# Forming three weight gradients per 512-token chunk between attention units, with fp32 sums in DRAM

## The chip, the cores and the metric

The kernel runs on one core of a Trainium2 chip. The metric is the device time of one execution, in microseconds (us). The kernel before takes 3382.19 us (median of 3 runs, 3378.85 to 3383.56). Runs of the same kernel in one job agree within about 0.3%. Between jobs the median of the kernel before ranged from 3380.52 to 3388.10 us, so times of different jobs are compared only where the difference is well above 8 us.

## The reference, cut to what matters

The kernel computes an adaptive-layernorm transformer block, its output and nine gradients. The sequence has 2048 tokens, the width is 512, there are 32 heads of 16, and the dense layer has 1792 hidden units.

```python
h = layernorm(x) * (1 + ca) + sa
x = x + ga * attention(h, wqkv, wo)
h = layernorm(x) * (1 + cb) + sb
x = x + gb * (relu(h @ w1 + b1) ** 2 @ w2 + b2)
# outputs: x and the gradients of A_x, wqkv, wo, w1, b1, w2, b2, c, w_mod
```

The change concerns the gradients of `wo` (output 3), `w1` (output 4) and `w2` (output 6). Each is a sum over all 2048 tokens.

## The kernel before

Forward attention is a list of 512 units: 4 query chunks of 512 tokens, 8 head groups, 16 key tiles. A unit is two pairs of score matmuls, two exponentials on ScalarE (ACT) and four matmuls with V ("PV"). Matmul results land in PSUM, in the profile lines below as tiles of 128x512 or 128x1024 fp32; a tile of 128x512 fills what I call one bank, and another engine has to copy it out ("evict" it) before the bank can be used again. When all head groups of a chunk are done, that chunk's dense forward and backward become a generator, and one step of it is put behind each unit of the next chunk. The last chunk's generator has no attention to hide behind; I call its run "the tail". "Stage J" is the stage that follows backward attention.

```python
pools["s"]  = tile_pool(name="psS", bufs=3, PSUM)   # scores, 2 banks each
pools["o"]  = tile_pool(name="psO", bufs=1, PSUM)   # PV sums
pools["mm"] = tile_pool(name="psM", bufs=1, PSUM)   # all dense work: one bank
with tc.manual_schedule(engines={PE.engine, ACT.engine}):
    for u in range(NF + 6):
        fscore(u)                 # scores and two exponentials
        fpv(u - 2)                # PV
        if dense:                 # one step of the chunk before
            if wait > 0: wait -= 1
            else: wait = next(dense[0], -1) ...
        # ffinish(...): normalise a finished chunk, start its generator
```

The dense steps store token-major copies of their operands (`gf_st`, `h2_st`, `da_st`, `stok_st`, `dztok_st`) in DRAM. After the tail comes a stage of its own:

```python
# load all stored operands; build padded, transposed weights for stage J
for t3 in range(3):
    for hg in range(HG):
        ...   # in all 96 small copies on ScalarE's DMA queue
        ACT.dma_start(out=wT_bld[o0:o0 + DH, ...], in_=tmpT[r0:r0 + DH, :])
for fc in range(FC):              # likewise for wo and w1
    acc = psg.tile([P, 512], F32, name="aw", tag="aw")
    for t in range(TT):           # sum over all 16 token tiles in PSUM
        PE.matmul(acc[:], sz["s", t // 4][:, fc, t % 4, :], toks["gf"][:, t, :],
                  start=(t == 0), stop=(t == TT - 1))
    acc_out(fc, wblk[:], acc[:])
    SP.dma_start(out=out_6[fc * P:(fc + 1) * P, :], in_=wblk[:])
```

Backward attention follows, then stage J, which uses the padded weights `wT_pad`.

## Time and profile before

The span of 3386.2 us splits as follows. The landmarks are the first score matmul, the last PV matmul, the first load for backward attention, and the last matmul of backward attention's dQ.

| stretch | us |
|---|---|
| preparation, to the first score | 287.1 |
| forward attention, first score to last PV | 991.8 |
| tail: dense work of the last chunk alone | 147.7 |
| weight-gradient stage, to the first backward load | 189.2 |
| backward attention | 1463.9 |
| the rest (stage J and the end) | 306.5 |

The first view is the busy-time windows of the kernel before. Columns: the window, the busy us of PE (TensorE), its weight load, DVE (VectorE), ACT and POOL (GpSimd), each with a count of instructions, then the granted clock, the DMA share and GB/s.

```profile
600.00:650.00 50.00, 44.78 (x313) 14.60 (x314) 18.67 (x33) 50.00 (x55) 8.45 (x7) 1.00 0.58 128
650.00:700.00 50.00, 45.57 (x304) 14.60 (x305) 21.50 (x55) 49.25 (x54) 11.84 (x23) 0.97 0.73 190
1500.00:1550.00 50.00, 13.39 (x49) 5.58 (x50) 2.08 (x3) 2.72 (x5) 0.00 (x0) 0.58 0.31 97
```

In the first two windows, attention with dense steps between units, ACT has almost no gap; TensorE is nearly as full. In the third, which holds the longest wait of the weight-gradient stage, every engine idles most of the time; over the whole stage TensorE is busy 115.8 of 189.2 us.

The chain of waits of the kernel before in a dense stretch (start, length, what) shows the second limit. L387 is the dense matmul group, L392 its eviction from PSUM.

```profile
590.12 0.76 DVE rT L392
590.88 0.04 issue
590.92 1.04 PE pm L387 x4
591.96 0.02 issue
591.99 0.76 DVE rT L392
```

One turn of the single dense bank is matmuls 1.04, a hand-over, eviction 0.76, a hand-over: 1.87 us from 590.12 to 591.99. That is as long as ACT's two exponentials, so one dense step per unit just fits.

The waits of the kernel before in the weight-gradient stage (who waits for whom: us in total, times, longest):

```profile
ACT wblk L641 <- DMA wT_bld<-tmpT: 80.5, 1, 80.5
PE aw L655 <- ACT wblk L641: 50.7, 1, 50.7
```

and its timeline there:

```profile
1448.82 16.28 PE L648 MATMUL aw<-da_g,O_g 128*128 128x512 bf16 x63 [41.64 <-DMA wT_bld<-tmpT]
...
1483.41 52.40 ACTq L636 DMA_DIRECT2D wT_bld<-tmpT  x80
```

TensorE waited 41.64 us for its first matmul of the stage. Later an eviction on ACT stood behind 80 small DMA issues (52.40 us; 16 of the 96 had gone out earlier), and TensorE waited 50.7 us for it.

The group of exponentials in forward attention, from the costliest groups (busy, mean ns, then the idle time ahead of them and what ended most of it):

```profile
L523 ACT ACTIVATE ET<-psST 128x1024 bf16<-128x1024 f32 x1024 | 945.5, 1311 | 34.7 <-PE psST L521 34.5
```

ACT waited only 34.5 us for scores in the whole forward attention.

### The profile page before, as it was taken

The page shows a single profiled execution, that of the slowest core. Times are in us where ns is not written, and L with a number is a line of the kernel's source. Part 1 is how long each engine was busy: PE and PEld are TensorE (multiplying, and loading weights), DVE is VectorE, ACT ScalarE, POOL GpSimd, SP SyncE. Part 2 cuts the span into 40 slices and gives each one's busy share as a digit, 9 for nine tenths or more (in the row PEclk, how much of TensorE's full clock was granted, in tenths as well). Part 3 has the DMA queues.
Part 4 walks back from the last instruction along what each step waited for, and adds up shares of the span by engine and source line. Part 5 has one row for each costly group of instructions (what it writes and reads, how often), then busy time and mean ns, then how long its engine had stood idle before and what let it go on. Part 6 is the DMA issues. An engine that isn't in the chain of part 4 may idle for free.

```text
span 3386.2 us, 47396 instructions
## 1 busy us (share of the span) xinstructions
PE 2663.9 (79%) x17485; PEld 788.3 (23%) x17549; DVE 1932.1 (57%) x2770; ACT 2157.3 (64%) x3474; POOL 372.3 (11%) x345
## 2 busy tenths in 40 slices
PE   2778998888888885348697889898898978885746
PEld 1232111221221222114122222222222222222312
DVE  8852002332343344400587878788887878884772
ACT  0006999999999992000586878787787868784202
POOL 3000001121121132300110010101010101010000
PEclk7986555975975976778788878888878889897867
DMA  3124001661662654763999999999999999997113
GB/s 128 55 107 150 29 29 47 136 173 52 138 166 57 137 155 100 167 211 115 219 200 213 199 211 197 207 205 204 208 198 209 198 215 201 201 201 182 63 62 94
DMA packets 1388742, 511.31 MB, mean 151 GB/s; under 512 B 1321939, under 2 KB 1359575, under 8 KB 1386205
## 3 DMA queue, kind: packets, MB, share of 16 engines
q1 hardware_dynamic: 1368782, 502.51, 70.8%
q10 hardware_dynamic: 19728, 5.77, 0.8%
q8 instruction: 138, 2.26, 0.3%
q14 instruction: 94, 0.77, 0.1%
HBM read 112.29 MB, written 74.08 MB: 55 GB/s over the span
## 4 chain that ended last, share of the span: by engine, by line
PE 36%; DMA 21%; ACT 18%; DVE 12%; issue 6%; SPq 3%; ACTq 2%; POOL 0%; DVEq 0%; POOLq 0%
DMA dsT<-dS_u 16%; ACT ET L523 14%; PE psS_u L724 7%; PE dqacc L776 5%; ACT E_u L726 4%; PE accVK L761 3%; PE ppad L266 3%; PE accVK L752 2%; PE psST L521 2%; DVE dS_u L738 2%; PE psS_x L724 2%; PE pm L387 2%; ACTq L636 1%; PE pm L420 1%; PE pm L403 1%
## 5 line engine op out<-in xcount | busy, mean ns | idle before, releaser
L738 DVE TENSOR_TENSOR dS_u<-psD_u,E_u 128x1024 bf16<-128x1024 f32 x1024 | 1189.4, 1218 | 248.5 <-PE psD_u L736 166.5
L726 ACT ACTIVATE E_u<-psS_u 128x512 bf16<-128x512 f32 x1536 | 866.3, 633 | 307.2 <-PE psD_u L736 274.0
L523 ACT ACTIVATE ET<-psST 128x1024 bf16<-128x1024 f32 x1024 | 945.5, 1311 | 34.7 <-PE psST L521 34.5
L724 PE MATMUL psS_u<-ik,iq 32*128 32x512 bf16 x1536 | 517.2, 434 | 27.0 <-DVE KS_tok L677 19.1
L521 PE MATMUL psST<-qt_sb,kt_sb 32*128 32x512 bf16 x2048 | 464.6, 507 | 85.2 <-ACT ET L523 37.7
L736 PE MATMUL psD_u<-iv,ido 32*128 32x512 bf16 x2048 | 448.4, 432 | 18.9 <-DVE dS_u L738 11.4
L776 PE MATMUL dqacc<-dsT,KS_tok 128*32 128x512 bf16 x2048 | 212.7, 503 | 161.0 <-DMA dsT<-dS_u 149.2
L726 ACT ACTIVATE E_u<-psS_x 128x512 bf16<-128x512 f32 x512 | 333.9, 652 | 2.2 <-PE psD_u L736 1.7
L537 PE MATMUL oacc<-ET,vaug 128*32 128x512 bf16 x2048 | 270.4, 517 | 0.6 <-ACT ET L523 0.6
L541 DVE COPY ostage<-oacc 128x512 f32<-128x512 f32 x32 | 22.0, 688 | 373.6 <-PE oacc L537 373.6
L761 PE MATMUL accVK<-E_u,dOs_tok 128*16 128x512 bf16 x2048 | 226.3, 432 | 0.0
L724 PE MATMUL psS_x<-ik,iq 32*128 32x512 bf16 x512 | 210.6, 411 | 0.6
L521 PEld LDWEIGHTS <-kt_sb 32*128 32x128 bf16 x2048 | 91.4, 96 | 461.7 <-issue 456.8
L724 PEld LDWEIGHTS <-iq 32*128 32x128 bf16 x2048 | 99.1, 93 | 378.6 <-issue 378.0
L736 PEld LDWEIGHTS <-ido 32*128 32x128 bf16 x2048 | 124.8, 93 | 228.4 <-issue 203.7
L791 POOL TENSOR_TENSOR dQacc<-dQacc,dqtmp 128x512 f32<-128x512 f32 x64 | 81.1, 1268 | 843.0 <-ACT dqtmp L786 843.0
L641 ACT ACTIVATE wblk<-aw 128x512 bf16<-128x512 f32 x9 | 5.4, 597 | 229.4 <-PE aw L648 125.2
L752 PE MATMUL accVK<-dS_u,qz_12652 128*32 128x512 bf16 x1024 | 113.1, 430 | 6.8 <-ACT vkb L764 5.8
L752 PE MATMUL accVK<-dS_u,qz_12651 128*32 128x512 bf16 x1024 | 112.0, 427 | 7.0 <-ACT vkb L764 6.1
L266 PE MATMUL ppad<-xn1T,wpadT 128*128 128x512 bf16 x376 | 98.7, 408 | 21.8 <-DVE stagep L269 16.2
L850 ACT ACTIVATE dqkv_tok<-ptq 128x64 bf16<-128x64 bf16 x128 | 28.6, 224 | 119.8 <-PE ptq L844 119.8
L776 PEld LDWEIGHTS <-KS_tok 128*32 128x32 bf16 x2048 | 52.1, 105 | 221.2 <-issue 179.0
(1021 smaller groups left out, 2496.9 us busy)
## 6 DMA issues: line engine op xcount, KB each, us to landing
kt_sb<-KtP SPq DMA_DIRECT2D x32, 512.0 KB, 3.7
dsT<-dS_u SPq DMA_TRANSPOSE x512, 5.1
wA<-in_B_w_dram SPq DMA_DIRECT2D x4, 1792.0 KB, 8.8
wB<-in_B_w_dram SPq DMA_DIRECT2D x4, 1792.0 KB, 7.7
stok_st<-tk SPq DMA_DIRECT2D x12, 512.0 KB, 3.0
dztok_st<-tk SPq DMA_DIRECT2D x12, 512.0 KB, 4.0
QtP<-stagep SPq DMA_DIRECT2D x8, 512.0 KB, 2.8
KtP<-stagep SPq DMA_DIRECT2D x8, 512.0 KB, 2.9
```

The costliest lines, as they stand in the source:

```text
L266: PE.matmul(pp[:], wpadT[:, ic, which, hg, :], h1T[:, ic, qc * 512:(qc + 1) * 512], start=(ic == 0), stop=(ic == DC - 1))
L521: PE.matmul(ps[:, hi, :], kt_sb[r:r + 32, kt * P:(kt + 1) * P], qt_sb[r:r + 32, :], start=True, stop=True, tile_position=(r, 0))
L523: ACT.activation(ET[:, 2 * pair:2 * pair + 2, :], ps[:], AF.Exp, scale=SCALE)
L537: PE.matmul(oacc[32 * hq:32 * hq + 32, :], lhsT, ET[:, hq, :], start=(kt == 0), stop=(kt == TT - 1), tile_position=(0, 32 * hq), skip_grou ...
L724: PE.matmul(psS[:], st["q"][r:r + 32, qt * P:(qt + 1) * P], st["k"][r:r + 32, kc * 512:kc * 512 + 512], start=True, stop=True, tile_positi ...
L726: ACT.activation(bst[u][0][:, hq, :], psS[:], AF.Exp, scale=SCALE)
L736: PE.matmul(psD[:, hi, :], st["do"][r:r + 32, qt * P:(qt + 1) * P], st["v"][r:r + 32, kc * 512:kc * 512 + 512], start=True, stop=True, til ...
L738: DVE.tensor_tensor(dS_u[:, 2 * pair:2 * pair + 2, :], psD[:], E_u[:, 2 * pair:2 * pair + 2, :], ALU.mult)
L752: PE.matmul(cur["vk"][32 * hq:32 * hq + 32, :], hst[hg]["qz"][:, qt, hq, :], bst[u][1][:, hq, :], start=(qt == 0), stop=False, tile_positi ...
L761: PE.matmul(acc[32 * hq:32 * hq + DH, :], dOs_tok[:, qt, (hg * 4 + hq) * DH:(hg * 4 + hq + 1) * DH], E_u[:, hq, :], start=False, stop=(qt ...
L776: PE.matmul(acc[32 * hq:32 * hq + 32, :], KS_tok[:, kc * 4 + kt, h * DH:h * DH + 32], tT[:, :, hq * 4 + kt, :], start=(kt == 0), stop=(kt ...
L791: POOL.tensor_tensor(dst2, dst, tmp[:], ALU.add)
```

## The change

The intent is to delete the weight-gradient stage. Each chunk's share of the three gradients is formed as 34 "pieces" (14 for `w2`, 16 for `w1`, 4 for `wo`) of 4 matmuls. They stand between the attention units, while operands are still in SBUF. Chunk 0 stores each piece in DRAM as fp32. Chunks 1 and 2 add to it by an accumulating DMA. Chunk 3, in the tail, loads the sum, adds its own share and writes the output. The padded weights of J come from 16 DMA transposes at the start of backward attention. Cut to its core:

```diff
+        def later(f, *args):
+            pend.append((clock[0] + 5, f, args))
+        def dw_piece(c, i, dst, ops, w):
+            if c == QC - 1:
+                part = wk.tile([P, 512], F32, name="dwp", tag="dwp", bufs=3)
+                SP.dma_start(out=part[:, 0:w], in_=dw_st[i][:, 0:w])
+            acc = mm()
+            for ti in range(4):
+                PE.matmul(acc[:, 0:w], ops[ti][0], ops[ti][1], start=(ti == 0), stop=(ti == 3))
+            if c == QC - 1:
+                res = wk.tile([P, 512], BF, name="dwr", tag="ta")
+                DVE.tensor_tensor(res[:, 0:w], acc[:, 0:w], part[:, 0:w], ALU.add)
+                SP.dma_start(out=dst, in_=res[:, 0:w])
+            else:
+                part = wk.tile([P, 512], F32, name="dwp", tag="dwp", bufs=3)
+                DVE.tensor_copy(part[:, 0:w], acc[:, 0:w])
+                if c == 0:
+                    POOL.dma_start(out=dw_st[i][:, 0:w], in_=part[:, 0:w])
+                else:
+                    POOL.dma_start(out=dw_st[i][:, 0:w], in_=part[:, 0:w], accum_op=ALU.add)
...
                 if fc % 4 == 3 or fc == FC - 1:
-                    to_tokens(sT, stok_st[c], fc // 4 * 4, fc + 1)
+                    tk = to_tokens(sT, f0, fc + 1)          # DMA transpose, no store
+                    for f in range(f0, fc + 1):
+                        later(dw_piece, c, DC + f, out_6[...], ..., D)
...
+                    clock[0] = u
+                    stepped = False
+                    if dense and wait == 0:
+                        stepped = True
+                        wait = next(dense[0], -1)
...
+                    if pend and pend[0][0] <= u and not open_group[0] and (not stepped or len(pend) > 2):
+                        _, f, args = pend.pop(0)
+                        f(*args)
...
-            for _ in vaug_left:
-                pass
+            while dense:                                    # the tail
+                for _ in dense.pop(0):
+                    if pend and not open_group[0]:
+                        _, f, args = pend.pop(0)
+                        f(*args)
...
-    (the whole weight-gradient stage)
...
+        for j in range(16):                                 # start of backward attention
+            SP.dma_start(out=wT_pad[:, j, :], in_=wpad_st[:, j * P:(j + 1) * P], transpose=True)
```

Not shown: longer-lived token-major tiles, four `tk` buffers instead of two, and the padded weights that are written to `wpad_st` during preparation.

More of the change, by code (lines that the diff above doesn't have):

```diff
@@ L90 @@
     dOs_st = dram.tile([P, TT, D], BF, name="dOs_st")
-    da_st = dram.tile([P, TT, D], BF, name="da_st")
-    h2_st = dram.tile([P, TT, D], BF, name="h2_st")
-    gf_st = dram.tile([P, TT, D], BF, name="gf_st")
     q_st = dram.tile([P, TT, QPAD], BF, name="q_st")
     k_st = dram.tile([P, TT, QPAD], BF, name="k_st")
-    stok_st = dram.tile([QC, P, 4 * FF], BF, name="stok_st")
-    dztok_st = dram.tile([QC, P, 4 * FF], BF, name="dztok_st")
-    wT_st = dram.tile([P, 16, D], BF, name="wT_st")
+    dw_st = dram.tile([DC + FC + 16, P, 512], F32, name="dw_st")
+    wpad_st = dram.tile([D, 16 * P], BF, name="wpad_st")
     QtP = dram.tile([HG, P, n], BF, name="QtP")
@@ L163 @@
             POOL.tensor_copy(dst, src)
+    wpadVK = wqkvpool.tile([P, DC, HG, 4, 2, DH], BF, name="wpadVK")
+    for ic in range(DC):
+        for t in (1, 2):
+            POOL.tensor_copy(wpadVK[:, ic, :, :, 2 - t, :],
+                             wqkv_nat[:, ic, t * 512:(t + 1) * 512].rearrange("p (hg h d) -> p hg h d", hg=HG, h=4))
+    wpad_v = wpad_st.rearrange("(ic p) c -> p ic c", p=P)
+    SP.dma_start(out=wpad_v[:, :, 0:HG * P], in_=wpadT[:, :, 0].rearrange("p i g c -> p i (g c)"))
+    SP.dma_start(out=wpad_v[:, :, HG * P:], in_=wpadVK.rearrange("p i g h v d -> p i (g h v d)"))
     sa_bc = modbc[:, 0, :]
@@ L321, in load_wB @@
             return w
+        pend, clock, open_group = [], [0], [False]
+        def later(f, *args):
[18 more added lines that the diff above has]
+                    POOL.dma_start(out=dw_st[i][:, 0:w], in_=part[:, 0:w], accum_op=ALU.add)
         def dense_chunk(c, O_c, act):
@@ L334, in dense_chunk @@
             SP.dma_start(out=OT.rearrange("p t o q -> p (t o) q"), in_=flat(O_c), transpose=True)
-            gf_c = cb.tile([P, 4, D], BF, name="gf_c", tag="hd")
+            gf_c = cb.tile([P, 4, D], BF, name="gf_c", tag="gf")
             POOL.tensor_tensor(gf_c[:], g_c[:], gb_bc.unsqueeze(1).to_broadcast([P, 4, D]), ALU.mult)
-            SP.dma_start(out=gf_st[:, ts, :], in_=gf_c[:])
             gfT = cb.tile([P, 4, DC, P], BF, name="gfT", tag="gfT")
@@ L370, in dense_chunk @@
                                   modcol[:, 4, ic:ic + 1], modcol[:, 3, ic:ic + 1], ALU.mult, ALU.add)
-            h2_c = cb.tile([P, 4, D], BF, name="h2_c", tag="hd")
+            h2_c = cb.tile([P, 4, D], BF, name="h2_c", tag="h2")
             POOL.tensor_tensor(h2_c[:], xn2_c[:], cb1_bc.unsqueeze(1).to_broadcast([P, 4, D]), ALU.mult)
             POOL.tensor_tensor(h2_c[:], h2_c[:], sb_bc.unsqueeze(1).to_broadcast([P, 4, D]), ALU.add)
-            SP.dma_start(out=h2_st[:, ts, :], in_=h2_c[:])
             yield 10
@@ L377, in dense_chunk, with to_tokens @@
             sT = cb.tile([P, FC, 512], BF, name="sT", tag="sT")
-            def to_tokens(src, dst, f0, f1):
-                tk = cb.tile([P, 16, P], BF, name="tk", tag="tk", bufs=2)
-                SP.dma_start(out=tk[:, 0:4 * (f1 - f0), :], in_=flat(src[:, f0:f1, :]), transpose=True)
-                SP.dma_start(out=dst[:, 512 * f0:512 * f1], in_=flat(tk[:, 0:4 * (f1 - f0), :]))
+            def to_tokens(src, f0, f1):
+                tk = cb.tile([P, 4, 4, P], BF, name="tk", tag="tk", bufs=4)
+                SP.dma_start(out=tk.rearrange("p f t q -> p (f t) q")[:, 0:4 * (f1 - f0), :], in_=flat(src[:, f0:f1, :]), transpose=True)
+                return tk
             for fc in range(FC):
@@ L394, in dense_chunk @@
                 if fc % 4 == 3 or fc == FC - 1:
-                    to_tokens(sT, stok_st[c], fc // 4 * 4, fc + 1)
+                    f0 = fc // 4 * 4
+                    tk = to_tokens(sT, f0, fc + 1)
+                    for f in range(f0, fc + 1):
+                        later(dw_piece, c, DC + f, out_6[f * P:(f + 1) * P, :],
+                              [(tk[:, f - f0, ti, :], gf_c[:, ti, :]) for ti in range(4)], D)
                 yield 0
@@ L404, in dense_chunk @@
                     if fc % 4 == 3:
+                        open_group[0] = True
                         yield 0
+                open_group[0] = False
                 PE.matmul(pf[:], ones_bf[0:1, 0:P], b2row[0:1, :], start=False, stop=True)
@@ L426, in dense_chunk @@
                 if fc % 4 == 3 or fc == FC - 1:
-                    to_tokens(dzT, dztok_st[c], fc // 4 * 4, fc + 1)
+                    f0 = fc // 4 * 4
+                    nf = fc + 1 - f0
+                    tk = to_tokens(dzT, f0, fc + 1)
+                    for ic in range(DC):
+                        later(dw_piece, c, DC + FC + 4 * (f0 // 4) + ic, out_4[ic * P:(ic + 1) * P, f0 * P:(fc + 1) * P],
+                              [(h2_c[:, ti, ic * P:(ic + 1) * P], tk[:, 0:nf, ti, :]) for ti in range(4)], nf * P)
                 yield 0
             yield 1
-            dx1_c = cb.tile([P, 4, D], BF, name="dx1_c", tag="od")
-            da_c = cb.tile([P, 4, D], BF, name="da_c", tag="hd")
+            dx1_c, da_c = g_c, a_c
             for ti in range(4):
@@ L438, in dense_chunk @@
                     if fc % 4 == 3:
+                        open_group[0] = True
                         yield 0
+                open_group[0] = False
                 xn2 = xn2_c[:, ti, :]
@@ L459, in dense_chunk @@
                                          op0=ALU.mult, op1=ALU.add)
-                DVE.tensor_tensor(da_c[:, ti, :], dx1_c[:, ti, :], ga_bc, ALU.mult)
                 proda = wk.tile([P, D], BF, name="proda", tag="tc")
                 DVE.tensor_tensor(proda[:], dx1_c[:, ti, :], a_c[:, ti, :], ALU.mult)
+                DVE.tensor_tensor(da_c[:, ti, :], dx1_c[:, ti, :], ga_bc, ALU.mult)
                 rowsum(3, proda[:], t)
@@ L467, in dense_chunk @@
             SP.dma_start(out=daT.rearrange("p t o q -> p (t o) q"), in_=flat(da_c), transpose=True)
-            SP.dma_start(out=da_st[:, ts, :], in_=da_c[:])
-            dOs_c = cb.tile([P, 4, D], BF, name="dOs_c", tag="od")
+            dOs_c = cb.tile([P, 4, D], BF, name="dOs_c", tag="x1_c")
             dOp = flat(cb.tile([P, FC, 512], BF, name="dOp", tag="sT"))[:, 0:4 * HG * P]
@@ L472, in dense_chunk @@
             POOL.memset(dOp, 0.0)
+            for oc in range(DC):
+                later(dw_piece, c, oc, out_3[oc * P:(oc + 1) * P, :],
+                      [(O_c[:, ti, oc * P:(oc + 1) * P], da_c[:, ti, :]) for ti in range(4)], D)
             yield 8
@@ L490, in dense_chunk @@
                 if ti % 2 == 1:
-                    dOT = cb.tile([P, 16, P], BF, name="dOT", tag="tk", bufs=2)
+                    dOT = cb.tile([P, 16, P], BF, name="dOT", tag="tk", bufs=4)
                     SP.dma_start(out=dOT[:], in_=dOp[:, ti - 1:ti + 1].rearrange("p t g c -> p (t g c)"), transpose=True)
@@ L539, in fpv @@
             if kt == TT - 1:
-                ostage = wk.tile([P, 512], F32, name="ostage", tag="ostage")
+                ostage = wk.tile([P, 512], F32, name="ostage", tag="ostage", bufs=1)
                 DVE.tensor_copy(ostage[:], oacc[:])
@@ L581 @@
                         fpv(u - 2)
-                    if dense:
-                        if wait > 0:
-                            wait -= 1
-                        else:
-                            wait = next(dense[0], -1)
-                            if wait < 0:
-                                dense.pop(0)
-                                wait = 0
-                    if fdone and (u - 2 >= fdone[0][0] or u == NF + 5):
+                    clock[0] = u
[3 more added lines that the diff above has]
+                        wait = next(dense[0], -1)
+                        if wait < 0:
+                            dense.pop(0)
+                            wait = 0
+                    elif wait > 0:
+                        wait -= 1
+                    if pend and pend[0][0] <= u and not open_group[0] and (not stepped or len(pend) > 2):
+                        _, f, args = pend.pop(0)
+                        f(*args)
+                    if not open_group[0] and fdone and (u - 2 >= fdone[0][0] or u == NF + 5):
                         ffinish(*fdone.pop(0)[1:])
-        vaug_left = dense.pop(0)
-        assert not dense
         with ExitStack() as ph2:
             pools["mm"] = ph2.enter_context(tc.tile_pool(name="psM2", bufs=8, space=bass.MemoryType.PSUM))
-            for _ in vaug_left:
-                pass
-            prows = wk.tile([1, D], F32, name="prows", tag="prows")
+            while dense:
[3 more added lines that the diff above has]
+                        f(*args)
+            for _, f, args in pend:
+                f(*args)
             for j, row in ((0, 5), (1, 3), (2, 4), (3, 2)):
@@ L601 @@
                 PE.matmul(pr[0:1, :], onesf[:, 0:1], racc[:, j, :], start=True, stop=True)
-                prows = wk.tile([1, D], F32, name="prows", tag="prows")
+                prows = wk.tile([1, D], F32, name="prows", tag="dwp", bufs=3)
                 DVE.tensor_copy(prows[:], pr[0:1, :])
@@ L609 @@
     vaugpool.release()
-    with ExitStack() as ph:
-        big = ph.enter_context(tc.tile_pool(name="phG", bufs=1))
-        wk = ph.enter_context(tc.tile_pool(name="phGw", bufs=2))
-        psg = ph.enter_context(tc.tile_pool(name="psG", bufs=8, space=bass.MemoryType.PSUM))
-        toks = {}
-        for key, src in (("gf", gf_st), ("O", o_st), ("da", da_st), ("h2", h2_st)):
-            toks[key] = big.tile([P, TT, D], BF, name=f"{key}_g")
-            SP.dma_start(out=toks[key][:], in_=src[:])
-        sz = {}
-        for key, src in (("s", stok_st), ("dz", dztok_st)):
-            for c in range(QC):
-                sz[key, c] = big.tile([P, FC, 4, P], BF, name=f"{key}{c}", tag="szc", bufs=6)
-                SP.dma_start(out=sz[key, c].rearrange("p f t q -> p (f t q)"), in_=src[c])
-        wT_bld = big.tile([P, 16, D], BF, name="wT_bld")
-        POOL.memset(wT_bld[:], 0.0)
-        for t3 in range(3):
-            for hg in range(HG):
-                if hg % 2 == 0:
-                    tmpT = wk.tile([P, D], BF, name="tmpT", tag="tmpT")
-                    SP.dma_start(out=tmpT[:], in_=A_wqkv[:, (t3 * 4 + hg // 2) * P:(t3 * 4 + hg // 2 + 1) * P], transpose=True)
-                for hq in range(4):
-                    r0 = (hg % 2) * 64 + hq * DH
-                    o0 = 32 * hq + (DH if t3 == 1 else 0)
-                    ACT.dma_start(out=wT_bld[o0:o0 + DH, (0 if t3 == 0 else 8) + hg, :], in_=tmpT[r0:r0 + DH, :])
-        ACT.dma_start(out=wT_st[:], in_=wT_bld[:])
-        def acc_out(i, dst, acc):
-            if i % 2 == 0:
-                ACT.activation(dst, acc, AF.Identity)
-            else:
-                DVE.tensor_copy(dst, acc)
-        for oc in range(DC):
-            acc = psg.tile([P, 512], F32, name="aw", tag="aw")
-            for t in range(TT):
-                PE.matmul(acc[:], toks["O"][:, t, oc * P:(oc + 1) * P], toks["da"][:, t, :], start=(t == 0), stop=(t == TT - 1))
-            wblk = wk.tile([P, D], BF, name="wblk", tag="wblk")
-            acc_out(oc, wblk[:], acc[:])
-            SP.dma_start(out=out_3[oc * P:(oc + 1) * P, :], in_=wblk[:])
-        for fc in range(FC):
-            acc = psg.tile([P, 512], F32, name="aw", tag="aw")
-            for t in range(TT):
-                PE.matmul(acc[:], sz["s", t // 4][:, fc, t % 4, :], toks["gf"][:, t, :], start=(t == 0), stop=(t == TT - 1))
-            wblk = wk.tile([P, D], BF, name="wblk", tag="wblk")
-            acc_out(fc, wblk[:], acc[:])
-            SP.dma_start(out=out_6[fc * P:(fc + 1) * P, :], in_=wblk[:])
-        for ic in range(DC):
-            accs = [psg.tile([P, 512], F32, name="aw", tag="aw") for j in range(4)]
-            for t in range(TT):
-                for j in range(4):
-                    nf = min(4, FC - 4 * j)
-                    PE.matmul(accs[j][:, 0:nf * P], toks["h2"][:, t, ic * P:(ic + 1) * P], sz["dz", t // 4][:, 4 * j:4 * j + nf, t % 4, :],
-                              start=(t == 0), stop=(t == TT - 1))
-            w1blk = wk.tile([P, FF], BF, name="w1blk", tag="w1blk")
-            for j in range(4):
-                nf = min(4, FC - 4 * j)
-                acc_out(j, w1blk[:, 512 * j:512 * j + nf * P], accs[j][:, 0:nf * P])
-            SP.dma_start(out=out_4[ic * P:(ic + 1) * P, :], in_=w1blk[:])
@@ L672 @@
+    jpool = tc.alloc_tile_pool(name="jpool", bufs=1)
+    wT_pad = jpool.tile([P, 16, D], BF, name="wT_pad")
     qpool = tc.alloc_tile_pool(name="qpool", bufs=1)
@@ L823 @@
         wk = ph.enter_context(tc.tile_pool(name="phJw", bufs=2))
-        wT_pad = bigJ2.tile([P, 16, D], BF, name="wT_pad")
-        SP.dma_start(out=wT_pad[:], in_=wT_st[:])
         dh1acc = bigJ2.tile([P, TT, D], F32, name="dh1acc")
@@ L909 @@
                     SP.dma_start(out=out_2[ic * P:(ic + 1) * P, t3 * D:(t3 + 1) * D], in_=wblk[:])
+    jpool.release()
     with ExitStack() as ph:
```

## The prediction

> **What bounds the kernel now.** By the busy-time windows and the timeline, the 3386 us span is: projections to 287 us; forward attention 287–1280; the last chunk's dense layers alone 1280–1425; weight-gradient stage 1427–1616; first backward scores at 1635, backward attention to about 3085; then the rest. Backward (DMA share above 1.1) is hardly touched. In forward attention ACT is busy 945 of 993 us: two 0.93 us exponentials per unit, 1.85 us. Where dense work runs between units TensorE is just as full: the timeline shows scores 0.33 + PV 0.33 + dense step 0.97 us, and the single PSUM bank of dense work turns round in 1.87 us (matmuls 1.02, DVE eviction 0.75, two hand-overs). Granted clock there is 1.0, with attention alone 0.50, the two values that the Trainium skill, "TensorE: Matmul & The Clock Gate", Part 1, gives.
>
> **Removed.** The stage 1427–1616, 189 us, all on the critical path: 41 us before its first matmul, a 51 us PE wait on an ACT copy stuck behind 80 small ACT DMA issues (waits view), about 110 us of matmuls. Also the 2 MB reload of J weights (est. 5 us).
>
> **Added, forward.** 34 pieces of 4 matmuls for each of chunks 0–2. By the instruction order, 25 of the 34 stand in a unit that already has a dense step, directly behind it, in the same PSUM bank. Such a unit costs scores and PV 0.66 + dense 1.02 + eviction wait about 0.85 + piece 0.97, and the piece's copy (0.69) gates the next: about 3.7 us instead of 1.85. In-order TensorE starves ACT. Estimate from these durations: 40–50 us a chunk, +135 us. The other 9 pieces cost nothing.
>
> **Added, tail.** Chunk 3's 34 pieces: 29 us of matmuls and 24 us of DVE adds, part hidden. The first piece of a transposed group stands directly behind the dense step that makes its last input; the transpose takes about 4.3 us to land, so about six stalls of 5 us. SP's queue mixes partial-sum loads and stores with those transposes. Estimate +55 us (30–80).
>
> **Moved.** 16 weight transposes (1.4 us issue each, from the timeline of the same shape) precede the first backward transposes: +8 us. More GpSimd copies and two stores early: +2 us.
>
> **Accumulating DMA.** The skill, "DMA: Bandwidth & Descriptors", Rules for kernel authors, puts accumulation on GpSimd; its fit for that path gives an estimated 2.6 us for 256 KB. Three buffers at 3.7 us a piece leave 11 us, so I expect no wait.
>
> **Sum.** 3382 − 189 − 5 + 135 + 55 + 8 + 2 = 3388; shaded to 3378, since some stalls may overlap. 80% range 3310 to 3440. Faster by over 2%: 0.16; within 2%: 0.73; slower: 0.11.
>
> **What would show it.** Forward: chunks 1–3 about 295 us each instead of 250; ACT busy share in dense windows falling from 1.0 to about 0.7; PE waits on the dwp copy and dense evictions; clock still 1.0; no dwp wait for DMA. Tail: about 200 us from last PV to the first backward load instead of 146, PE waits on tk transposes. Backward start about 8 us later relative to its loads, its length unchanged.
>
> **What would make it wrong.** Faster if evictions end sooner than I read or PE's lead absorbs more: forward under +80 us, result near 3310. Slower if accumulating DMAs land late (over 11 us) and hold up DVE, or if stalls drop the clock to 0.5.

## The result, and the profile after

The changed kernel is correct and takes 3424.36 us (median of 4 runs, 3421.42 to 3426.49). The kernel before took 3380.52 us in the same job. The ratio is 1.0129, with a 95% interval of 1.0111 to 1.0146: 1.3% slower, which counts as the same at a threshold of 2%. A ratio is the mean time of one kernel's fast runs over that of the other's of the same rounds, so it is not quite the ratio of the medians quoted.

| stretch, us | before | after | difference | predicted |
|---|---|---|---|---|
| preparation | 287.1 | 284.8 | −2.3 | +2 |
| forward attention | 991.8 | 1128.6 | +136.8 | +135 |
| tail | 147.7 | 233.6 | +85.9 | +55 |
| weight-gradient stage | 189.2 | – | −189.2 | −189 |
| backward attention | 1463.9 | 1476.2 | +12.3 | +8 |
| the rest | 306.5 | 299.9 | −6.6 | −5 |
| span | 3386.2 | 3423.1 | +36.9 | +6, shaded to −4 |

A removed stage of 189 us came back as 137 us inside forward attention and 86 us in the tail.

The windows of the changed kernel, in the same columns as before:

```profile
600.00:650.00 50.00, 40.82 (x254) 13.52 (x253) 19.15 (x31) 34.82 (x38) 8.06 (x13) 0.97 0.53 132
650.00:700.00 50.00, 38.34 (x231) 12.45 (x229) 17.86 (x38) 32.98 (x35) 12.35 (x23) 0.93 0.52 121
```

ACT's share fell from 1.00 and 0.98 to 0.70 and 0.66. TensorE is less busy than before as well, so neither engine is the limit by its work. The chain of waits of the changed kernel in such a stretch says what is (L415 dense matmuls, L420 their eviction, L340 the piece's matmuls, L347 its copy out of PSUM):

```profile
609.46 1.04 PE pm L340 x4
610.50 0.02 issue
610.52 0.70 DVE dwp L347
611.22 0.04 issue
611.26 1.04 PE pm L415 x4
612.30 0.03 issue
612.33 0.76 DVE rT L420
613.09 0.04 issue
613.13 1.04 PE pm L340 x4
```

A unit now takes two turns of the one dense bank: 3.67 us, from 609.46 to 613.13, instead of 1.87. In this trace the matmuls start in the order of the program: the scores of the next unit start at 610.41 us, behind the piece that had waited 0.84 us for the bank until 609.46. So ACT gets them late. The group of exponentials shows it:

```profile
L565 ACT ACTIVATE ET<-psST 128x1024 bf16<-128x1024 f32 x1024 | 951.7, 1275 | 165.2 <-PE psST L563 164.7
```

Its busy time is unchanged within 7 us, and its wait for scores grew from 34.5 to 164.7 us: 130 of the 137 us. By the start times of the matmuls in the trace, 66 units (22 a chunk) hold both a dense matmul and a piece, with a median of 3.69 us; the attention of chunks 1 to 3 took 295, 299 and 299 us, where the kernel before took 253, 251 and 253.

In the tail, the timeline of the changed kernel shows the longest stall, first on the sync engine's DMA queue (SPq):

```profile
1516.49 7.65 SPq L322 DMA_TRANSPOSE wB<-in_B_w_dram  x6
1524.24 0.52 SPq L448 DMA_DIRECT2D out_dram<-x_c  x1
1524.81 10.75 SPq L322 DMA_TRANSPOSE wB<-in_B_w_dram  x8
1535.65 1.95 SPq L409 DMA_TRANSPOSE tk<-rT  x1
```

and then on TensorE:

```profile
1540.06 1.87 PE L340 MATMUL pm<-tk,h_c 128*128 128x512 bf16 x4 [20.59 <-DMA tk<-rT]
```

The transpose that feeds the first `w1` piece stood behind 14 weight transposes, and TensorE waited 20.59 us. The six other stalls of this kind are 5.79, 5.99, 6.05, 0.70, 5.42 and 5.70 us, about 50 us together.

### The profile page after: what moved, and what is told of

It is laid out like the page before. It is cut to its first block, busy times and chain, and to the rows that moved or that the text cites. A ratio compares the mean times of both kernels' runs of the same rounds, so it can differ in the third digit from the quotient of the medians.

```text
span 3423.1 us, 47777 instructions
## 1 busy us (share of the span) xinstructions
PE 2663.0 (78%) x17549; PEld 782.0 (23%) x17549; DVE 2001.8 (58%) x2889; ACT 2153.1 (63%) x3457; POOL 448.2 (13%) x454
## 4 chain that ended last, share of the span: by engine, by line
PE 38%; DMA 20%; ACT 17%; DVE 14%; issue 7%; SPq 3%; POOL 0%; DVEq 0%; POOLq 0%; ACTq 0%
DMA dsT<-dS_u 15%; ACT ET L565 12%; PE psS_u L714 6%; PE dqacc L766 5%; ACT E_u L716 4%; PE pm L340 3%; PE accVK L751 3%; PE ppad L270 2%; PE accVK L742 2%; DVE dS_u L728 2%; PE psST L563 2%; PE psS_x L714 2%; PE pm L415 2%; PE pm L435 2%; PE pm L454 2%
## 5 line engine op out<-in xcount | busy, mean ns | idle before, releaser
L565 ACT ACTIVATE ET<-psST 128x1024 bf16<-128x1024 f32 x1024 | 951.7, 1275 | 165.2 <-PE psST L563 164.7
L563 PE MATMUL psST<-qt_sb,kt_sb 32*128 32x512 bf16 x2048 | 427.8, 501 | 66.2 <-ACT ET L565 22.3
L563 PEld LDWEIGHTS <-kt_sb 32*128 32x128 bf16 x2048 | 83.0, 95 | 425.4 <-issue 423.0
L347 DVE COPY dwp<-pm 128x512 f32<-128x512 f32 (+1 forms) x102 | 67.1, 658 | 103.1 <-PE pm L340 82.5
L340 PE MATMUL pm<-tk,h_c 128*128 128x512 bf16 (+1 forms) x256 | 64.8, 379 | 72.9 <-DMA tk<-rT 41.1
L270 PE MATMUL ppad<-xn1T,wpadT 128*128 128x512 bf16 x384 | 97.0, 401 | 21.0 <-DVE stagep L273 16.3
L340 PE MATMUL pm<-gf_c,tk 128*128 128x512 bf16 x224 | 65.6, 421 | 56.9 <-DMA tk<-sT 18.5
```

The costliest lines, as they stand in the source:

```text
L270: PE.matmul(pp[:], wpadT[:, ic, which, hg, :], h1T[:, ic, qc * 512:(qc + 1) * 512], start=(ic == 0), stop=(ic == DC - 1))
L340: PE.matmul(acc[:, 0:w], ops[ti][0], ops[ti][1], start=(ti == 0), stop=(ti == 3))
L563: PE.matmul(ps[:, hi, :], kt_sb[r:r + 32, kt * P:(kt + 1) * P], qt_sb[r:r + 32, :], start=True, stop=True, tile_position=(r, 0))
L565: ACT.activation(ET[:, 2 * pair:2 * pair + 2, :], ps[:], AF.Exp, scale=SCALE)
```

## The experiments

All use the landmarks of the table above. "Last PV to load" is the tail, and for kernels that still have the weight-gradient stage it includes that. The border between it and "backward" is the first load, and in some kernels the loads behind it come up to 13 us later. So I also read from last PV to the first dQ matmul where it matters: 377.7 us before, 280.9 after, 246.8 in e2.

| kernel | start | forward | last PV to load | backward | rest | span |
|---|---|---|---|---|---|---|
| before | 287.1 | 991.8 | 336.9 | 1463.9 | 306.5 | 3386.2 |
| after | 284.8 | 1128.6 | 233.6 | 1476.2 | 299.9 | 3423.1 |
| e1_own_unit | 287.7 | 1033.0 | 251.5 | 1481.0 | 297.8 | 3351.0 |
| e2_lag | 290.0 | 1128.0 | 192.6 | 1480.5 | 302.0 | 3393.1 |
| e3_own_lag | 290.5 | 1032.4 | 212.1 | 1483.2 | 301.0 | 3319.2 |
| e4_banks | 289.6 | 1099.6 | 232.6 | 1478.1 | 300.8 | 3400.7 |
| e5_before_banks | 286.2 | 1043.4 | 336.6 | 1461.4 | 306.3 | 3433.9 |
| e6_no_accum | 288.6 | 1115.7 | 232.1 | 1475.3 | 297.8 | 3409.5 |
| e7_one_mm | 286.7 | 1104.2 | 234.0 | 1476.5 | 300.8 | 3402.2 |
| e8_wt_late | 285.6 | 1128.7 | 233.5 | 1480.8 | 301.1 | 3429.7 |
| e9_alternate | 290.4 | 1020.7 | 207.1 | 1486.5 | 297.7 | 3302.4 |
| e10_alternate_actq | 287.8 | 1022.6 | 201.0 | 1483.5 | 297.1 | 3292.0 |
| e11_own_no_accum | 288.7 | 1015.2 | 247.5 | 1478.1 | 298.0 | 3327.5 |
| e12_sync_queue | 287.9 | 1024.3 | 182.3 | 1484.5 | 299.4 | 3278.4 |

My theory: forward loses its time because a unit with a dense step and a piece turns the one dense PSUM bank twice; the tail loses it in transposes that were asked for too late. The rivals for forward are the accumulating DMA holding up the buffers, and the plain extra work of matmuls on TensorE.

### e1_own_unit: a piece takes a unit of its own

```diff
-                    stepped = False
-                    if dense and wait == 0:
-                        stepped = True
+                    if pend and pend[0][0] <= u and not open_group[0]:
+                        _, f, args = pend.pop(0)
+                        f(*args)
+                        wait = max(wait - 1, 0)
+                    elif dense and wait == 0:
                         wait = next(dense[0], -1)
...
-                    if pend and pend[0][0] <= u and not open_group[0] and (not stepped or len(pend) > 2):
-                        _, f, args = pend.pop(0)
-                        f(*args)
```

Two planned waits of the generator were cut (`yield 6` to 5, `yield 10` to 7) so that a chunk still fits into 128 units.

> Change: in forward attention a weight-gradient piece takes a unit of its own (the dense step waits one unit), never the same unit as a dense step; two waits of the dense layers are shortened by 1 and 3 units so that all fits. Same matmuls, copies and accumulating DMAs. Theory (the piece queues behind the dense step for the one PSUM bank, 3.67 us a unit instead of 1.85, 25 times a chunk): forward attention falls from 1129 us to 995-1015, total about 3300. Rival 1 (the extra DVE copies and accumulating DMAs hold the pipeline up): they are all still there, forward falls by less than 40 us.

Measured: 3354.64 us median, ratio to before 0.9906 (0.9891 to 0.992). Forward fell by 95.6 us to 1033.0. The same pieces, with the same matmuls and DMAs, cost 41 us over the kernel before instead of 137. So sharing a unit was the main cost, and the work itself was not. The result still missed the expected 995 to 1015, and the total missed the expected 3300. The waits of this kernel in forward attention show one that was 20.4 us in the changed kernel and has doubled:

```profile
DVE dwp L347 <- DMA dw_st<-dwp: 39.7, 21, 6.6
```

Pieces that come in successive units use the three `dwp` buffers again after about 5.5 us (3 units of 1.85), and the accumulating DMA has often not landed by then. e11 and e9 test this. The tail grew by 18 us: the last steps of chunk 2 now end so late that they run past the last PV and hold up the tail's start.

### e2_lag: in the tail, a piece waits until its transpose has had time

```diff
+            lag[0] = 10
             while dense:
                 for _ in dense.pop(0):
-                    if pend and not open_group[0]:
+                    clock[0] += 1
+                    if pend and pend[0][0] <= clock[0] and not open_group[0]:
```

`later` uses `lag[0]`, which is 5 until the tail.

> Change: only after attention has ended (last chunk), a piece is issued at the earliest 10 steps after the dense step that makes its operand, instead of directly behind it. Theory (the tail grew by 86 us mainly because TensorE stands 50 us waiting for seven transposes of the operand, one of them 20.6 us behind 14 weight transposes on SP's queue): from last PV to first backward load falls from 234 us to 180-195, total about 3375-3385, forward unchanged. Rival (the tail's growth is the extra matmuls, adds and SP issues themselves): under 15 us gained, the waits reappear elsewhere.

Measured: 3394.84 us, ratio 1.002 (1.0005 to 1.0035). The tail fell by 41.0 us to 192.6, as expected, and forward stayed at 1128.0; the total missed the expected 3375 to 3385. About 7 of the 41 us were lost again right behind the border: the loads that follow the first one go out up to 12 us after it, and TensorE waited 11.8 us for one of them (`ik`). From last PV to the first dQ matmul the gain is 34.1 us. This is what the Trainium skill, "DMA: Bandwidth & Descriptors", Rules for kernel authors, advises: issue the DMA early, do other work, wait for it late. The 50 us of stalls for the pieces' transposes are gone from the tail's waits, but one wait took some of it over, as the rival had said:

```profile
PE pm L520 <- DMA daT<-a_c: 36.5, 1, 36.5
```

This wait was 4.3 us in the changed kernel and 20.7 in the kernel before.

### e3_own_lag: both

The edits of e1 and e2 together.

> Both of the first two. If they are separate causes the gains add: about 3424 - 125 - 45 = 3254, range 3235-3280, faster than the kernel before by 3 to 4%. If they share a cause, the sum falls short by over 20 us.

Measured: 3320.71 us (3316.25 to 3326.49), ratio 0.9803 (0.9786 to 0.982), about 2% below the kernel before (at a threshold of 2% the verdict is "unclear"; e1 was already below both kernels, by less). The span is 103.9 us below that of the changed kernel; e1 alone gave 72.1 and e2 alone 30.0, so the two gains add. It missed the expected time because e1 had.

### e4_banks and e5_before_banks: three dense banks instead of one

The pools of forward attention already take 6 + 1 + 1 banks of PSUM, as many as the tail's own pool of 8, so the banks come from the scores. e4 is the changed kernel with this edit, e5 the kernel before with the same edit, as its control.

```diff
-            pools["s"] = ... name="psS", bufs=3 ...
+            pools["s"] = ... name="psS", bufs=2 ...
-            pools["mm"] = ... name="psM", bufs=1 ...
+            pools["mm"] = ... name="psM", bufs=3 ...
```

> Change: the changed kernel with 3 PSUM banks for dense steps and pieces instead of 1, taken from attention's score buffers (2 pairs instead of 3). The pieces stay in the units of the dense steps. Theory (the wait for the bank is 0.85 + 0.2 of the 1.82 us that such a unit loses): the unit shrinks to about 2.6 us, forward attention falls by 60-80 us; some of it may be lost to the shorter score buffering. Rival 2 (it is the extra matmul time alone): forward unchanged or longer.

> Control for the run with 3 dense PSUM banks: the kernel BEFORE with the same split (2 score pairs, 3 dense banks). Tells what the shorter score buffering costs by itself; I expect forward attention within -15 to +25 us of the 993 us of before.

Measured: e4 3400.03 us, ratio 1.0034; e5 3435.64 us, ratio 1.0146 (1.0131 to 1.0161). Both missed. Forward of e4 fell by only 29 us, and forward of e5 rose by 51.6 us: the new split cost far more than I had expected. In chunk 0, where no dense step runs and only the two score buffers can matter, it cost 8.7 us (235.1 to 243.8, in e4 and e5 alike). Read against its own control, e4 pays 1099.6 − 1043.4 = 56 us for the pieces, where the changed kernel pays 137. So with three banks 81 us of the cost are gone. That is a difference of two kernels that each contain the second effect. The unit itself is the more direct reading. The timeline of TensorE in e4 (612 to 640 us) shows the pieces of successive units (L340) 2.49 us apart, where the changed kernel has 3.67:

```profile
618.06 1.03 PE L340 MATMUL pm<-gf_c,tk 128*128 128x512 bf16 x4
620.55 1.03 PE L340 MATMUL pm<-gf_c,tk 128*128 128x512 bf16 x4
```

Over all 66 units that hold both, the median fell from 3.69 to 2.70 us (expected about 2.6) and the sum from 260 to 202 us. So the theory held for the unit; what it did not foresee is what the other units lost with two score buffers.

### e6_no_accum: the accumulating DMAs left out (wrong)

```diff
-                else:
-                    POOL.dma_start(out=dw_st[i][:, 0:w], in_=part[:, 0:w], accum_op=ALU.add)
```

> Wrong result on purpose: the changed kernel without the accumulating DMAs of chunks 1 and 2 (copies to SBUF stay). Theory: forward unchanged, the stretch of units for chunks 1 and 2 (attention of chunks 2 and 3) within 5 us of the changed kernel's. Rival 1 (accumulating DMAs press back through the three buffers and DVE): over 15 us shorter per chunk.

Measured: forward 1115.7, 13 us less than with them; the outputs 3, 4 and 6 are wrong. I had expected a change within 5 us. The accumulating DMA costs the changed kernel something, but about a tenth of the 137 us. The attention of chunks 2 and 3, where it runs, became 6.8 and 8.2 us shorter; the rival had said over 15 each.

### e7_one_mm: pieces of one matmul instead of four in chunks 0 to 2 (wrong)

```diff
-            for ti in range(4):
-                PE.matmul(..., start=(ti == 0), stop=(ti == 3))
+            for ti in range(4 if c == QC - 1 else 1):
+                PE.matmul(..., start=(ti == 0), stop=(ti == (3 if c == QC - 1 else 0)))
```

> Wrong result on purpose: the changed kernel with one matmul per piece instead of four in chunks 0-2; copies, DMAs and order stay. Theory (the bank's round trip costs more than the matmuls): the unit that holds both falls by 3 x 0.216 = 0.65 us, forward attention by 45-50 us of its 137. Rival 2 (the extra matmul time is the cost): forward falls by about three quarters of the 137, over 95 us.

Measured: forward fell by 24 us. Three quarters of the pieces' matmul work removed gave a sixth of the cost back, so TensorE's work as such is refuted as the main cause. The gain is also half of what I had expected. A unit with both did fall, from 3.67 to 3.02 us (in the timeline, pieces start at 612.82 and 615.84), and the 66 units that hold both fell by 42 us in all. But the 141 units with a dense step alone took 25 us longer, 324.5 instead of 299.5. Their mean granted clock was 0.82, against 0.88 in the changed kernel; those of them at full clock took 1.90 us on average in both kernels, but 51 were below full clock instead of 26. The windows of e7 show such a stretch:

```profile
650.00:700.00 50.00, 37.20 (x205) 10.54 (x205) 16.65 (x37) 30.55 (x32) 11.71 (x23) 0.78 0.54 121
700.00:750.00 50.00, 39.46 (x268) 12.34 (x268) 26.75 (x62) 45.05 (x48) 22.34 (x27) 0.94 0.59 170
```

From 650 to 700 us the granted clock is 0.78, where the changed kernel has 0.93 (though the two kernels are not at the same units there). So in this one run, whose state is unknown, the missing gain goes with a lower clock; that the smaller pieces lowered it was not shown by a second run. The Trainium skill, "TensorE: Matmul & The Clock Gate", "A second HAM failure mode: psum-queue depth-cycling", describes a kernel whose clock swings because TensorE idles briefly between groups that cycle through PSUM. That resembles this; no run here shows that it is the same thing.

### e8_wt_late: the 16 weight transposes moved from the start of backward attention to stage J

The loop of 16 transposes stands ahead of `dh1acc` in stage J instead of after `load_head(0)`.

> Change: the 16 transposes of the J weights are issued before stage J instead of before the backward attention. Theory (they hold up the first backward transposes; from first backward load to last dq matmul is 12 us longer than before): that stretch is 8-12 us shorter, and stage J starts later by up to 25 us, so the total is the same or up to 15 us longer. If the backward start does not shorten, the 12 us have another cause.

Measured: 3431.69 us, ratio 1.0131. The first dQ matmul came 37.8 us after the first backward load, against 47.3 in the changed kernel and 40.8 before. But the whole stretch took 1480.8 us, no less than the 1476.2 of the changed kernel. Where the transposes ran, the tile view of `wT_pad` says (duration in ns min/median/max, then first and last start in us), in e8 and then in the changed kernel:

```profile
L815 SPq DMA_TRANSPOSE wT_pad<-wpad_st x16: 1255/1260/1836, 1671.0 to 1712.8; - x16
L787 SPq DMA_TRANSPOSE wT_pad<-wpad_st x16: 1258/1259/9516, 1649.9 to 1678.8; - x16
```

So they did not move to stage J. They still ran inside backward attention, now between its own transposes `dsT<-dS_u`, the first of which was issued at 1668.37 us instead of 1680.13. The transposes do delay the start: without them ahead of it the first dQ matmul came 9.5 us earlier. But from the first to the last dQ matmul e8 then took 1443.0 us, against 1428.9 in the changed kernel and 1423.2 before. A backward attention free of these transposes was not run, so whether they explain the longer stretch is not tested.

### e9_alternate: e3, with pieces and dense steps in turn

```diff
+                    turn = pend and pend[0][0] <= u and not open_group[0] and not (last[0] and dense and wait == 0)
+                    last[0] = turn
-                    if pend and pend[0][0] <= u and not open_group[0]:
+                    if turn:
```

> As e3 (own unit plus the tail's lag), but a piece may not follow a piece while a dense step is ready: they alternate, so that the next use of the same partial-sum buffer comes about 11 us later instead of 5.5, and the chunk's work is over before the next chunk starts. Theory (the rest of the cost in e1 and e3 is back-pressure from the accumulating DMA on runs of pieces in successive units): VectorE's wait on that DMA falls from about 40 us to under 8, the forward stretch from 1032 to 995-1012 us, the tail from 212 to 190-198 (nothing spills past the last PV), span 3265-3295. Rival (the rest is the piece itself: a PE unit of its own already costs about 0.4 us each): forward unchanged at 1025-1040, span 3300-3325.

Measured: 3298.67 us, ratio 0.9744 (0.9728 to 0.9761). Forward fell by 12 us to 1020.7, which lies between the theory's 995 to 1012 and the rival's 1025 to 1040, so it supports the theory in direction only. The span, 3302.4, falls on the rival's side (3300 to 3325). The wait on the accumulating DMA in forward attention of e9 is now

```profile
DVE dwp L348 <- DMA dw_st<-dwp: 11.8, 4, 4.2
```

after 32.9 us in e3. The tail, 207.1, missed its 190 to 198. In e9 the first reciprocal of the last head group's sums starts 18.5 us after the last PV (1311.1 to 1329.6), against 5.6 in the changed kernel (1413.4 to 1419.0): its small DMAs stood on the sync queue behind the stores of the chunk before. e12 tests that.

### e10_alternate_actq: e9, with the tail's output stores on ScalarE's queue

```diff
-                SP.dma_start(out=dst, in_=res[:, 0:w])
+                ACT.dma_start(out=dst, in_=res[:, 0:w])
```

> As e9, but the tail's 34 stores of finished gradients go out on ScalarE's queue (idle in the tail) instead of the sync engine's, so that a partial-sum load or a transpose never stands behind a store that waits for VectorE. Theory (in the tail the sync queue's mixed loads, stores and transposes hold up VectorE and TensorE): tail 8 to 20 us shorter than e9, forward equal within 5. Rival (the tail is bound by its own chain of dense steps and pieces on TensorE): tail equal within 4 us.

Measured: 3293.79 us, ratio 0.9737 (0.9722 to 0.9751). The tail fell by 6.1 us, between the theory's 8 to 20 and the rival's 4, and the interval overlaps that of e9. So the theory did not hold in its size, and no gain of e10 over e9 is shown by the times.

### e11_own_no_accum: e1 without the accumulating DMAs (wrong)

The edit of e6 on e1.

> Wrong on purpose: e1 with the accumulating DMAs of chunks 1 and 2 left out (chunk 0's plain stores stay), so the two summed terms are missing in three weight gradients. Theory (back-pressure of the accumulating DMA is what e1 fell short by): forward 1033 falls to 995-1010. Rival (it is the pieces on TensorE, or the spilled steps): forward 1025 or more.

Measured: forward 1015.2, 17.8 us less than e1, between the theory and the rival. VectorE's wait for that DMA in forward attention is

```profile
DVE dwp L347 <- DMA dw_st<-dwp: 3.1, 2, 2.3
```

so the wait is gone, and with it 18 of the 41 us that e1 pays. The other 23 us have another cause; the trace has one wait of that size, TensorE's for the transposes `tk<-rT` (23.3 us, 3 times), which no run removed. The DMA view of the changed kernel (kind, count, size, median us from issue to landing) shows why the wait is there. While chunk 0's pieces are stored (590 to 790 us):

```profile
dw_st<-dwp POOLq DMA_DIRECT2D x30, 256.0 KB, 2.8
```

and while chunk 1's are added (840 to 1090 us):

```profile
dw_st<-dwp POOLq DMA_DIRECT2D x30, 256.0 KB, 4.7
```

Here the accumulating DMAs took 1.9 us longer to land than the plain ones of the same size. In e1 the medians are 2.8 and 5.1 us.

### e12_sync_queue: e10, with two kinds of DMA taken out of the sync queue's way

```diff
-            w1T = load_wB(True)
+            w1T = ffw.tile([P, FC, D], BF, name="wB", tag="wB")
...                                               # in the loop over fc:
+                SP.dma_start(out=w1T[:, fc, :], in_=B_w1[:, fc * P:(fc + 1) * P], transpose=True)
...
-                        SP.dma_start(out=dOtP[hg]..., in_=dOT...)
+                        POOL.dma_start(out=dOtP[hg]..., in_=dOT...)
```

> As e10, with two edits that only move work off the in-order sync queue, each read at its own place. (a) The 14 transposed loads of w1T are issued one per dense step of the dz loop instead of all before it, so that the first tk<-rT transpose of a chunk no longer stands behind 14 of them. (b) The 8 dOtP stores of each dOT go out on GpSimd's queue, so that the rrows DMAs of a finished head group no longer stand behind them. Theory (what keeps the forward stretch at 1020 against 992 of before, apart from the accumulating DMA, is TensorE waiting for transposes held up in that queue): PE's waits on tk<-rT in the forward stretch fall from 15.5 us to under 4, on dOtP from 8.6 to under 2; forward 1022 to 995-1008 us. The time from the last PV matmul to the first reciprocal of the last head group falls from 22 us (e9: 1311.1 to 1329.6 and on) to 8-14; tail 201 to 180-192; span 3255-3278. Rival (the rest of the forward cost is the pieces' share of TensorE and the 0.2 us hand-overs): forward 1016 or more although the waits on tk are gone. If the tail's daT wait (37 us in e10) or the partial-sum loads simply take over the time won, the tail stays at 198-204.

Measured: 3280.74 us, ratio 0.9701 (0.9685 to 0.9717): 3.0% faster than the kernel before, 4.2% faster than the changed kernel (3280.74 over 3424.36, medians of different jobs), and the best of all. The span, 3278.4, is at the edge of the expected 3255 to 3278. The parts came out differently. The tail fell by 18.7 us to 182.3, as expected; the time from last PV to the first reciprocal fell from 18.6 us in e10 to 11.9 (1312.2 to 1324.1), which is about 7 of these. Forward did not move, although edit (b) removed its waits for `dOtP` stores (8.6 us in e10). The wait that edit (a) was to remove is still there:

```profile
PE pm L341 <- DMA tk<-rT: 15.7, 3, 5.3
```

The timeline of the sync queue in e12 says why:

```profile
660.45 18.32 SPq L468 DMA_TRANSPOSE wB<-in_B_w_dram  x13
678.87 4.58 SPq L410 DMA_TRANSPOSE tk<-rT  x2
```

Only PE and ACT are ordered by hand in forward attention. The order of the sync queue is worked out by the scheduler, which again put 13 weight transposes in a row ahead of `tk<-rT`. My edit did not change what it was meant to change. So its theory is not tested for forward, and its rival is not either.

## Why the prediction was right or wrong

The prediction was 3378 us with a range of 3310 to 3440, and 0.73 for "within 2%". The result, 3424.36 us at a ratio of 1.0129, lies in the range and within 2%. Point by point:

- **The limit, right.** Forward attention was bound by ACT, with the one dense bank turning in about the same 1.87 us. In the profiled runs the clock fell to 0.97 and 0.93 in two windows; "clock still 1.0" was nearly right. The two values 0.50 and 1.0 that it took from the skill ("TensorE: Matmul & The Clock Gate", Part 1) are what the trace shows: the kernel before was granted 1.0 for 1901 us and 0.5 for 1460 us, and no other value.
- **The removed stage, right.** 189.2 us went.
- **Forward, right in mechanism and size.** Predicted +135, measured +136.8; a unit with both took 3.67 us, predicted about 3.7; chunks 1 to 3 took 295, 299 and 299 us, predicted about 295; ACT's share fell to 0.70 and 0.66, predicted 0.7. e1 shows that sharing the unit was the main cost (−95.6 us). e4 shows that the bank is what was shared (the unit fell to a median of 2.70 us with three banks). e7 refutes the matmul work itself as the main cost. That the total fits within 2 us is partly luck: 22 pieces a chunk, not 25, share a bank with a dense matmul, which at 1.85 us each makes about 122 us, and the rest came from terms that the prediction had put at nothing, the accumulating DMA (13 us by e6) among them.
- **"No dwp wait for DMA", wrong in part.** VectorE waited 20.4 us (10 times) for the accumulating DMA in forward attention, and e6 prices it at 13 us. The estimate of 2.6 us, from the fit in the skill's "DMA: Bandwidth & Descriptors", holds for plain stores (2.8 us measured). It does not hold for accumulating ones (4.7 us median in chunk 1). "Three buffers at 3.7 us a piece leave 11 us" is true of a median, and where pieces stood in successive units the time left was half of it.
- **The tail, mis-sized: this is the term that was off.** Predicted +55, measured +85.9. "About six stalls of 5 us" were seven stalls with 50 us in all, because one was 20.6 us long, behind 14 weight transposes on the same queue. A further 11 us was one VectorE wait for an output store, in the loop of loads, adds and stores. These two make up the missing 31 us in sum, but that is arithmetic and not a test: the second was only read from the trace, and other waits of the tail changed too (for `daT`, from 20.7 us before to 4.3). e2 shows that most of the stalls were avoidable: −41.0 us in the tail, −34.1 to the first dQ matmul.
- **Backward, right at the start, wrong in "its length unchanged".** Predicted +8, measured +12.3. The first dQ matmul came 6.5 us later after the first load, near the predicted 8, and e8 shows that the transposes hold it up. The other 5.8 us lie between the first and the last dQ matmul (1428.9 us, before 1423.2), and their cause stays open: e8 did not take the transposes out of that stretch. All kernels with the change need 1475 to 1487 us, the two without it 1461 and 1464; part of that spread lies between the first load and the first dQ matmul (37.8 to 56.4 us).
- **Preparation and J.** Predicted +2 and −5, measured −2.3 and −6.6. Neither matters.
- **Shading the sum** from 3388 down to 3378 "since some stalls may overlap" was a guess in the wrong direction.

So where did the gain of 189 us go? 137 us went into forward attention, most of it waits of TensorE on one PSUM bank, which starved ACT, and 86 us became a longer tail, about half of it waits for transposes. Both come mostly from where the pieces were put, not from their number. With pieces in units of their own, in turn with dense steps, and late enough in the tail, the same change gives 2.6% (e9), and 3.0% with some DMAs moved out of the sync queue's way (e12).

What stays open: of the 32 us that forward attention in e12 still costs over the kernel before, the trace names three waits for `tk` transposes (15.7 us together) and 16.3 us of VectorE's waits for the accumulating DMA. No run took the first away. In the tail of e12 the longest wait of TensorE is 32.9 us for the transpose `daT`, and no run went after it. The longer backward stretch is unexplained.

## What to carry to other kernels

Filling idle engine time does not make work free: a unit that is bound by one engine may also be exactly full in a shared resource, here a PSUM bank that turns once per unit, and a second user doubles the unit. Give added work a slot of its own, spread it so that its buffers have time to come free, and put it late enough for its DMA to have landed. Before trusting a reordering of DMA issues, look whether the queue's order in the trace has changed: the source order need not be it (e8 and e12).

## What the Trainium skill lacked or had wrong

- "DMA: Bandwidth & Descriptors", "Anatomy of one DMA — SWDGE (gpsimd) path": the fit gives an estimated 2.6 us for 256 KB. Plain stores agree (2.8 us median of 30). Accumulating stores of the same size on the same queue took 4.7 us in chunk 1 and 4.8 in chunk 2. Neither the fit nor the rules give a figure for accumulation.
- The same page gives no figure for how long a DMA transpose of this size holds the issuing queue on this chip. Here 13 weight transposes kept the sync queue busy for 18.32 us, 1.4 us each, and what stood behind such a row waited: 20.59 us of TensorE in the tail of the changed kernel.
- "TensorE: Matmul & The Clock Gate": it has no figure for what the clock does when matmuls are taken out of a kernel bound by hand-overs. In e7, a single run, the mean clock in units with a dense step alone was 0.82 instead of 0.88 when the pieces shrank from four matmuls to one, and these units took 25 us longer in all.
- No page that I used says what a shorter score buffer costs when the exponentials are the limit: two buffers instead of three cost 8.7 us in chunk 0 (e5), and together with the three dense banks 51.6 us in forward attention.
